# Where the first gate piece of a unit stands among the score products of a fused attention and feed-forward kernel

## The chip, the cores and the metric

The kernel runs on one core of a Trainium2 chip. The metric is the device time of one execution in microseconds (us); lower is better. Before the change the median of three executions is 332.06 us (331.29 to 332.46). The profiled execution took 331.38 us, and its trace spans 329.6 us from the first to the last instruction.

The engines are named as in the profile: PE is TensorE's matmuls, PEld its weight loads, ACT is ScalarE, DVE VectorE, POOL GpSimd, SP the engine that issues most transfers. L347 is line 347 of the kernel.

## The reference

An attention whose tokens attend only to tokens of the same cluster (the cluster of a token is the nearest of 16 centroids), followed by a SwiGLU feed-forward block on the normalised result. Four batches, 8 heads, 768 tokens, head size 64; model width 512, inner width 1536.

```python
q_assign = argmax(einsum('bhsd,hcd->bhsc', q_n, c_n), axis=-1)      # q_n, k_n, c_n: normalised rows
k_assign = argmax(einsum('bhsd,hcd->bhsc', k_n, c_n), axis=-1)
mask = q_assign[:, :, :, None] == k_assign[:, :, None, :]
scores = where(mask, scale * (q @ k.T), -1e9)
attn = softmax(scores)
x = (attn @ v)                       # reshaped to 3072 tokens x 512

xn = x / sqrt(mean(x * x) + 1e-6) * rms_g
g = xn @ w_gate
out = (g * sigmoid(g) * (xn @ w_val)) @ w_out
```

## The kernel before

The work is cut into 8 units, numbered 0 to 7: unit `u` is half of the query tokens (384) of one batch, for all 8 heads. A head of a unit has three *gaps*; in each, one pair of score matmuls is issued and its exponential taken. The one-hot cluster of a token is appended to its query and key (80 rows instead of 64), so that the mask comes out of the score product itself.

```python
def scores(u, h, i):
    ...
    ps = ps_s.tile([P, 2, 512], F32, tag="s", name="s")          # ps_s has 2 buffers in PSUM
    for j in range(n):                                            # n = 2: the pair
        nc.tensor.matmul(ps[:, j, :w], lhsT=cols(kext...), rhs=cols(qext...), start=True, stop=True)   # L347
    nc.scalar.activation(pT[u, h][:, n * i:n * i + n, :w], of, ACT.Exp, bias=off, ...)                # L351
```

`pv(u, h)` multiplies the exponentials of a finished head with the values (18 matmuls with 65 columns, L365), and after every second head normalises the result into `x` on VectorE (L370, L372). It runs one head late, after the second score pair of the next head. At a seam between units it is therefore the last head of unit `u - 1` that is multiplied after the second pair of unit `u`.

While the last head of a unit runs, ScalarE also squares the finished columns of `x` for the mean square, one of three pieces in each gap (`squares`, L392).

The feed-forward block of an earlier unit is cut into pieces. A gate or a value piece is four matmuls of 384 columns, into one of three PSUM buffers:

```python
def gv(u, f, val):
    ...
    full = ps_g.tile([P, UQ], F32, tag="gen", name="val" if val else "gate")    # ps_g has 3 buffers in PSUM
    for c in range(CC):
        nc.tensor.matmul(ps, lhsT=w[:, c, f * P:(f + 1) * P], rhs=xnT[u][:, c, :n], ...)               # L443
    if not val:
        th = gate.tile([P, UQ], F32, tag="th", name="th")[:, :n]
        nc.scalar.activation(th, ps, ACT.Tanh, scale=0.5)                                             # L451
        nc.vector.scalar_tensor_tensor(th, th, 1.0, ps, op0=ALU.add, op1=ALU.mult)                    # L452
    else:
        nc.vector.scalar_tensor_tensor(gvT[u][:, f, :n], gates[u], 0.5, ps, ...)                      # L456
```

(The last unit's gate and value products take another form; it is cut here.) The output product of a finished unit is cut into pieces in the same way (`out_mm`, L468), and the cluster products of the next group of heads too (L253).

`attention` writes the program of a unit: in each of its 24 gaps a score pair, in some a `pv`, and then pieces from the list `fill`, each with an estimated cost, so that they are spread evenly over the gaps:

```python
def attention(heads, fill, skip=0, hooks={}):
    gaps = [(u, h, i) for u, h in heads for i in range(UNITS[u][2])]
    total, done, n = sum(c for c, _ in fill), 0.0, 0
    for at, (u, h, i) in enumerate(gaps):
        scores(u, h, i)
        if i == (0 if (u, h) == (1, 0) else 1):
            for p in due:
                pv(*p)
            due[:] = [(u, h)]
        if h == H - 1:
            squares(u, i, False)
        ...
        while n < len(fill) and at >= skip and done <= total * (at + 1 - skip) / (len(gaps) - skip):
            done += fill[n][0]
            fill[n][1]()
            n += 1
```

From unit 2 on, `fill` begins with the last 8 gate and value pieces of unit `u - 2`; after them come the normalising of unit `u - 1`, the output pieces of unit `u - 2`, work for the next group of heads, and the first 16 gate and value pieces of unit `u - 1`. Units 2 to 5 skip the first gap, units 6 and 7 don't:

```python
    fill = ffn_work(u - 2)[CUT:] + [(0.0, lambda u=u: rms(u - 1))]                # CUT = 16 of 24
    rows, clusters = group(g)                                                     # g = u + 2
    ...
    attention([(u, h) for h in range(H)], fill, 1 if g < NG else 0)               # NG = 8
```

PE, ACT and DVE each take their instructions in the order in which the program issues them. The one-hot rows of a later group of heads are brought to their places in `kext` and `qext` by transfers that POOL issues (L296), behind a chain on DVE (cluster products transposed, the largest found, compared, transposed back).

Of the kernel before, what the change touches and what calls it, by code (L numbers as in the profile page):

```python
# [22 lines left out]
def kernel(  # L23
# [13 lines left out]
    B, H, S, D = q.shape  # L37
# [8 lines left out]
    NG = B * H // HG  # L46
# [158 lines left out]
    def load_o(c):  # L205
        nc.gpsimd.dma_start(out=wo[:, c:c + 4], in_=moe_w_out[c * P:(c + 4) * P].rearrange("(c p) f -> p c f", p=P))
# [130 lines left out]
    def scores(u, h, i):  # L337
        b, col, nt = UNITS[u]
        g, hh, w = b * 2 + h // HG, h % HG, nt * P
        if i == 0:  # L340
            pT[u, h] = ptp.tile([P, ST, UQ], BF16, tag="pT", name="pT")
        n = ST // nt
        ps = ps_s.tile([P, 2, 512], F32, tag="s", name="s")
        flat = ps.rearrange("p a b -> p (a b)")
        for j in range(n):
            kc = n * i + j
            nc.tensor.matmul(ps[:, j, :w] if nt == HT else flat[:, j * w:(j + 1) * w],  # L347
                             lhsT=cols(kext[g % 4][:KR, hh], g, kc // HT, kc % HT * P, (kc % HT + 1) * P),
                             rhs=cols(qext[g % 4][:KR, hh], g, col // HT, 0, w), start=True, stop=True)
        of = ps[:, :, :w] if nt == HT else flat[:, :n * w].rearrange("p (c w) -> p c w", w=w)  # L350
        nc.scalar.activation(pT[u, h][:, n * i:n * i + n, :w], of, ACT.Exp, bias=off, scale=scale if g >= BG else scale * ZS)  # L351
# [3 lines left out]
    def pv(u, h):  # L355
        b, _, nt = UNITS[u]
        g, hh = b * 2 + h // HG, h % HG
        if h == 0:
            xs[u] = xp.tile([P, HT, DM], F32, tag="x", name="x", bufs=2)
        if h % 2 == 0:  # L360
            accs[u] = ps_a.tile([P, 2, HT, D + 1], F32, tag="acc", name="acc")
        acc = accs[u]
        for t in range(nt):
            for kc in range(ST):
                nc.tensor.matmul(acc[:, h % 2, t], lhsT=pT[u, h][:, kc, t * P:(t + 1) * P],  # L365
                                 rhs=vbf[g % 4][:, hh, kc % HT * 2 + kc // HT], start=kc == 0, stop=kc == ST - 1)
        if h % 2:
            inv = small.tile([P, 2, HT], F32, tag="inv", name="inv")
            invs[u] = inv
            nc.vector.reciprocal(inv[:, :, :nt], acc[:, :, :nt, D])  # L370
            dst = xs[u][:, :nt, (h - 1) * D:(h + 1) * D].rearrange("p t (h d) -> p h t d", d=D)
            nc.vector.tensor_tensor(dst, acc[:, :, :nt, :D],  # L372
                                    inv[:, :, :nt].unsqueeze(3).broadcast_to([P, 2, nt, D]), op=ALU.mult)
# [8 lines left out]
    def squares(u, t, last):  # L382
        if (t, last) == (0, False):
            sq[u] = small.tile([P, 2, HT], F32, tag="ss", name="ss")
            xn[u] = xp.tile([P, CC, HT, P], BF16, tag="xn", name="xn")
        c = slice(CC - 1, CC) if last else slice(0, CC - 1)
        x, junk = by_chunk(xs[u][:, t])[:, c], xn[u][:, c, t]
        to = sq[u][:, int(last), t:t + 1]
        if u == 0:
            nc.vector.scalar_tensor_tensor(junk, x, 1.0 / DM, x, op0=ALU.mult, op1=ALU.mult, accum_out=to)  # L390
        else:
            nc.scalar.activation(junk, x, ACT.Square, scale=DM ** -0.5, accum_out=to)  # L392
# [95 lines left out]
    def group_work(g):  # L488

        t, c = [], []  # L490
        for h in range(HG):
            n = g * HG + h
            w = 0.0 if g >= BG else 0.3
            t += [(w, lambda h=h: trans(g, h, 0)), (w, lambda h=h: trans(g, h, 1))]

            def others(n=n):
                vcast(n)
                if n + NQ not in LATE:
                    load_qk(n + NQ)
                load_v(n + AV)  # L500

            def both(h=h, f=others):
                cast(nc.gpsimd, g, h, 0)
                f()
                cast(nc.gpsimd if g >= BG else nc.vector, g, h, 1, (0,))
            if g == 2:
                c.append((0.0, others))
            else:
                c += [(0.0, both), (0.0, lambda h=h: cast(nc.gpsimd if g >= BG else nc.vector, g, h, 1, (1,)))]
        a = []  # L510
        for m in range(2):
            a += [(0.0 if i else 0.7, f) for i, f in enumerate(cluster_steps(g, m))]
            if g == 3:
                a.append((0.0, lambda m=m: place(nc.gpsimd, g, m)))
            elif g == 2:
                a.append((0.0, (lambda: (place(nc.gpsimd, g, 1), place(nc.gpsimd, g, 0, (1,)))) if m else
                          (lambda: place(nc.gpsimd, g, 0, (0,)))))
        if g > 3:
            a[:1] = [(1.4, lambda f=(a[0][1], a.pop(4)[1]): [x() for x in f])]
            a.append((0.0, lambda: [place(nc.gpsimd, g, m) for m in range(2)]))  # L520
        return t, c, a

    def weave(t, c):

        return [x for pair in zip(t, c) for x in pair] + c[len(t):]
# [8 lines left out]
    def spread(a, b):  # L534

        if not a:
            return list(b)
        w, n = [], 0
        for i, x in enumerate(a):
            w.append(x)  # L540
            while n < len(b) * (i + 1) // len(a):
                w.append(b[n])
                n += 1
        return w

    def ffn_work(u):
        n = UNITS[u][2] / HT
        return [(0.64 * n, lambda f=f, val=val: gv(u, f, val)) for f in range(FC) for val in (False, True)]

    def out_work(u):  # L550
        return [(0.86, lambda t=t, p=p: out_mm(u, t, p)) for t in range(UNITS[u][2]) for p in range(3)]
# [103 lines left out]

    due = []

    def attention(heads, fill, skip=0, hooks={}):
        gaps = [(u, h, i) for u, h in heads for i in range(UNITS[u][2])]
        total, done, n = sum(c for c, _ in fill), 0.0, 0  # L660
        for at, (u, h, i) in enumerate(gaps):
# [6 lines that stand above are left out]
                squares(u, i, False)  # L668
            if (u, h, i) in hooks:
                hooks[u, h, i]()  # L670
            while n < len(fill) and at >= skip and done <= total * (at + 1 - skip) / (len(gaps) - skip):
                done += fill[n][0]
                fill[n][1]()
                n += 1
        for _, f in fill[n:]:
            f()

    attention([(0, h) for h in range(H)], [], hooks={(0, *divmod(i, HT)): f for i in range(H * HT) for f in [first.get(i, more)] if f})
    for u in range(1, NU):
        ffn, o, g = ffn_work(u - 1), out_work(u - 2) if u > 1 else [], u + 2  # L680
        if u == 1:
            t, c, a = group_work(2)
            t3, c3, a3 = group_work(3)
            n = LEAD - 4
            o3 = [(0.0, lambda i=i: load_o(i)) for i in range(0, FC, 4)]
            prep = c + a + spread(weave(t3[n:], c3), o3) + a3[:5]
            idle = const.tile([P, 1], BF16)

            def norm():
                rms(0)  # L690
                nc.gpsimd.tensor_copy(idle, xn[0][:, CC - 1, HT - 1, P - 1:])
                for h in range(HG):
                    casts(pool_, H + h, K0, Q0, K1, Q1)

            hooks = {(1, 0, 0): late[6], (1, 0, 1): lambda: (late[7](), norm())}
            hooks.update({(1, *divmod(2 + i, HT)): t3[i][1] for i in range(n)})
            hooks[1, *divmod(LEAD - 1, HT)] = lambda: xtrans_all(0)
            fill = spread(ffn[:CUT], prep)
            attention([(1, h) for h in range(H)], fill, LEAD, hooks)
        else:  # L700
            fill = ffn_work(u - 2)[CUT:] + [(0.0, lambda u=u: rms(u - 1))]
            rows, clusters = group(g)
            fill += [(0.0, lambda n=n: load_qk(n)) for n in LATE if n // HG == u + 3]
            if u == 2:
                fill += spread(o[:3], [(0.0, f) for _, f in a3[5:]])
                o = o[3:]
            fill += spread(o, rows) + spread(ffn[:CUT], clusters)
            attention([(u, h) for h in range(H)], fill, 1 if g < NG else 0)
    rest = ffn_work(NU - 2)[CUT:]
    rest[0][1]()  # L710
    pv(NU - 1, H - 1)
# [38 lines left out]
```

The softmax here doesn't subtract the row's maximum and nothing guards it: scores larger than these inputs give would overflow.

## Time and profile before

| | before |
|---|---|
| median of 3 executions | 332.06 us |
| span of the trace | 329.6 us |
| PE busy | 320.9 us (97%) |
| ACT busy | 247.8 us (75%) |
| DVE busy | 223.7 us (68%) |
| POOL busy | 136.3 us (41%) |
| DMA, mean over the span | 104 GB/s |
| matmuls | 2877 |

A busy time is the sum of the intervals in which an engine has an instruction recorded. A group line of the page names the line, the engine, the operation, what it writes and reads, and how many there are; behind the bar stand the busy time, the mean duration of one in ns, and the idle time of the engine just before these instructions with what ended it. A line of a timeline gives the start and the length in us, then the engine, the line, the operation and how many in a row were merged; in brackets stands the idle time before it and what ended it.

The chain of waits that ended last lies on PE for 77% of the span, on DVE for 10% and on ACT for 6%.

### The profile page before, as it was taken

How to read it: one execution, taken by the hardware profiler on the slowest of the kernel's cores; microseconds unless marked ns; L12 is line 12 of the kernel's file. 1: busy time of each engine (PE TensorE's matmuls, PEld its weight loads, DVE VectorE, ACT ScalarE, POOL GpSimd, SP SyncE). 2: the span in 40 equal slices, each digit the busy share in tenths (PEclk: the TensorE clock that was granted, in tenths of full speed). 3: DMA queues.
4: the chain of work that ended last, by engine and by line, in shares of the span. 5: the costliest groups of instructions: out<-in, count | busy, mean ns of one | idle time of the engine just before them, and what ended most of it. 6: DMA issues, size and time to landing. Idle time of an engine off the chain costs nothing.

```text
span 329.6 us, 7822 instructions
## 1 busy us (share of the span) xinstructions
PE 320.9 (97%) x2877; PEld 192.8 (58%) x2877; DVE 223.7 (68%) x508; ACT 247.8 (75%) x429; POOL 136.3 (41%) x273
## 2 busy tenths in 40 slices
PE   8999899999999999999999999999999999999995
PEld 4647557564466655665566555665566656655653
DVE  6999976968777685877678694976265635684430
ACT  5899979986679867897778876797779868853331
POOL 6999499950977156440926247350000000000000
PEclk9999999999999999999999999999999999999999
DMA  7999995894546344561546640000600040002002
GB/s 266 367 263 241 255 201 108 129 198 112 89 92 142 104 69 74 118 150 52 97 74 131 161 111 34 6 21 1 146 2 0 2 111 34 2 1 95 2 1 97
DMA packets 82919, 34.25 MB, mean 104 GB/s; under 512 B 64064, under 2 KB 79808, under 8 KB 82880
## 3 DMA queue, kind: packets, MB, share of 16 engines
q1 hardware_dynamic: 73712, 27.44, 34.4%
q0 software_dynamic: 8880, 5.91, 10.9%
q8 instruction: 23, 0.38, 0.5%
q10 hardware_dynamic: 288, 0.39, 0.4%
q14 instruction: 16, 0.13, 0.1%
HBM read 28.61 MB, written 6.29 MB: 106 GB/s over the span
## 4 chain that ended last, share of the span: by engine, by line
PE 77%; DVE 10%; ACT 6%; SPq 3%; issue 2%; DMA 1%; POOL 0%; DVEq 0%; ACTq 0%; POOLq 0%
PE o L468 18%; PE gate L443 15%; PE val L443 15%; PE s L347 15%; PE acc L365 8%; ACT pT L351 3%; SPq L95 3%; PE sc L253 2%; DMA qk<-in_k_dram 1%; ACT xn L392 1%; ACT th L451 1%; DVE kext L331 1%; DVE qext L331 1%; PE warm L131 1%; DVE pads L326 1%
## 5 line engine op out<-in xcount | busy, mean ns | idle before, releaser
L351 ACT ACTIVATE pT<-s,off 128x768 bf16<-128x768 f32 x192 | 171.0, 905 | 32.2 <-PE s L347 31.6
L347 PE MATMUL s<-qext,kext 80*128 80x384 bf16 x384 | 94.8, 328 | 2.7 <-ACT pT L351 1.9
L443 PE MATMUL gate<-xnT,wg 128*128 128x384 bf16 x384 | 78.3, 326 | 0.1
L443 PE MATMUL val<-xnT,wv 128*128 128x384 bf16 x384 | 78.1, 326 | 0.0
L452 DVE SCALAR_TENSOR_TENSOR th<-th,gate 128x384 f32<-128x384 f32 x84 | 46.2, 550 | 36.6 <-ACT th L451 36.1
L468 PE MATMUL o<-wo,gvT 128*128 128x512 bf16 x276 | 68.1, 379 | 0.0
L347 PEld LDWEIGHTS <-kext 80*128 80x128 bf16 x384 | 36.3, 98 | 37.0 <-issue 9.1
L456 DVE SCALAR_TENSOR_TENSOR gvT<-th,val 128x384 bf16<-128x384 f32 x84 | 46.5, 553 | 10.2 <-PE val L443 3.1
L451 ACT ACTIVATE th<-gate 128x384 f32<-128x384 f32 x84 | 41.2, 490 | 15.1 <-PE gate L443 14.3
L443 PEld LDWEIGHTS <-wg 128*128 128x128 bf16 x384 | 36.0, 97 | 23.0 <-issue 0.8
L365 PEld LDWEIGHTS <-pT 128*128 128x128 bf16 x1152 | 43.4, 97 | 10.0 <-DVE x L372 1.1
L443 PEld LDWEIGHTS <-wv 128*128 128x128 bf16 x384 | 36.0, 97 | 22.4
L239 POOL CAST qext<-qkT 64x384 bf16<-64x384 f32 x64 | 35.5, 561 | 32.7 <-DVE inv L370 20.4
L365 PE MATMUL acc<-vbf,pT 128*128 128x65 bf16 x1152 | 45.7, 193 | 0.6 <-ACT pT L351 0.2
L468 PEld LDWEIGHTS <-gvT 128*128 128x128 bf16 x276 | 25.8, 97 | 26.0 <-issue 0.6
L296 POOL DMA_DIRECT2D qext<-oh x48 | 23.1, 491 | 27.0 <-DVE oh L285 22.5
L239 POOL CAST kext<-qkT 64x384 bf16<-64x384 f32 x54 | 29.4, 545 | 4.0 <-DVE qkT L224 2.2
L296 POOL DMA_DIRECT2D kext<-oh x48 | 23.0, 488 | 14.7 <-DVE oh L285 14.6
L471 ACT COPY o_sb<-o 128x512 f32<-128x512 f32 x23 | 13.5, 586 | 15.8 <-PE o L468 15.8
L370 DVE RECIPROCAL inv<-acc 128x6 f32<-128x6 f32 x32 | 6.0, 189 | 22.6 <-PE acc L365 22.0
L372 DVE TENSOR_TENSOR x<-acc,inv 128x384 f32<-128x384 f32 x32 | 17.8, 557 | 1.1
L242 POOL CAST vbf<-vs 128x384 bf16<-128x384 f32 x32 | 16.6, 527 | 1.6
(83 smaller groups left out, 235.4 us busy)
## 6 DMA issues: line engine op xcount, KB each, us to landing
vs<-in_v_dram SPq DMA_DIRECT2D x32, 192.0 KB, 4.2
out_dram<-o_sb SPq DMA_DIRECT2D x23, 256.0 KB, 2.5
qk<-in_q_dram SPq DMA_DIRECT2D x16, 192.0 KB, 4.2
qk<-in_q_dram SPq DMA_DIRECT2D x64, 48.0 KB, 2.7
qk<-in_k_dram SPq DMA_DIRECT2D x64, 48.0 KB, 2.6
qk<-in_k_dram SPq DMA_DIRECT2D x14, 192.0 KB, 4.4
wg<-in_moe_w_gate_dram POOLq DMA_DIRECT2D x4, 384.0 KB, 8.8
wv<-in_moe_w_val_dram POOLq DMA_DIRECT2D x4, 384.0 KB, 11.4
```

The source lines that it names most:

```text
L239: on.tensor_copy(to, of)
L242: nc.gpsimd.tensor_copy(vbf[n // HG % 4][:, n % HG, :, :D], stagedv[n])
L296: on.dma_start(out=ext[D:D + NC, h, e * UQ:(e + 1) * UQ], in_=put[g, m][32 * h + e * NC:32 * h + (e + 1) * NC])
L347: nc.tensor.matmul(ps[:, j, :w] if nt == HT else flat[:, j * w:(j + 1) * w], lhsT=cols(kext[g % 4][:KR, hh], g, kc // HT, kc % HT * P, (kc ...
L351: nc.scalar.activation(pT[u, h][:, n * i:n * i + n, :w], of, ACT.Exp, bias=off, scale=scale if g >= BG else scale * ZS)
L365: nc.tensor.matmul(acc[:, h % 2, t], lhsT=pT[u, h][:, kc, t * P:(t + 1) * P], rhs=vbf[g % 4][:, hh, kc % HT * 2 + kc // HT], start=kc == 0 ...
L372: nc.vector.tensor_tensor(dst, acc[:, :, :nt, :D], inv[:, :, :nt].unsqueeze(3).broadcast_to([P, 2, nt, D]), op=ALU.mult)
L443: nc.tensor.matmul(ps, lhsT=w[:, c, f * P:(f + 1) * P], rhs=xnT[u][:, c, :n], start=c == 0, stop=c == CC - 1)
L451: nc.scalar.activation(th, ps, ACT.Tanh, scale=0.5)
L452: nc.vector.scalar_tensor_tensor(th, th, 1.0, ps, op0=ALU.add, op1=ALU.mult)
L456: nc.vector.scalar_tensor_tensor(gvT[u][:, f, :n], gates[u], 0.5, ps, op0=ALU.mult, op1=ALU.mult)
L468: nc.tensor.matmul(outs[u], lhsT=gvT[u][:, f, t * P:(t + 1) * P], rhs=wo[:, f], start=f == 0, stop=f == FC - 1)
```

## The change

The change gives `attention` a new argument, `ahead`: that many pieces of `fill` may be issued before the skipped gaps are over. With `ahead=1`, the first piece of units 2 to 5 (a gate piece of unit `u - 2`) is issued in the first gap, between the first two score pairs of the unit, where before nothing stood between them. It is there to give PE work while the second pair waits for its buffer.

```diff
-    def attention(heads, fill, skip=0, hooks={}):
+    def attention(heads, fill, skip=0, hooks={}, ahead=0):
...
-            while n < len(fill) and at >= skip and done <= total * (at + 1 - skip) / (len(gaps) - skip):
+            while n < len(fill) and (n < ahead or at >= skip) and done <= total * (at + 1 - skip) / (len(gaps) - skip):
...
-            attention([(u, h) for h in range(H)], fill, 1 if g < NG else 0)
+            attention([(u, h) for h in range(H)], fill, 1 if g < NG else 0, ahead=1)
```

On PE the four gate matmuls of each of the four units move ahead of the second score pair and the `pv` behind it. On ACT the tanh of that gate comes between the first two exponentials of the unit, where it came behind the second. On DVE its product comes ahead of the reciprocal and the normalising of `x` instead of behind them. The programs of POOL and SP are the same.

## The prediction

> **What bounds the kernel now.** I read the page first for the engines' shares, then a table of stages, then the timelines of TensorE (PE) and ScalarE (ACT) at the seams between two units. The page:
>
> ```profile
> PE 320.9 (97%) x2877; PEld 192.8 (58%) x2877; DVE 223.7 (68%) x508; ACT 247.8 (75%) x429; POOL 136.3 (41%) x273
> L351 ACT ACTIVATE pT<-s,off 128x768 bf16<-128x768 f32 x192 | 171.0, 905 | 32.2 <-PE s L347 31.6
> L347 PE MATMUL s<-qext,kext 80*128 80x384 bf16 x384 | 94.8, 328 | 2.7 <-ACT pT L351 1.9
> ```
>
> TensorE is the busy engine, and the exponentials of ScalarE wait for it (31.6 us in all) far more than it waits for them (1.9 us). That 1.9 us is the change's target. A matmul's recorded end is modelled, so its busy share flatters it; I therefore go by starts. Four 384-column matmuls of a gate or value piece start 0.65 us before the next group (gate at 105.40, val at 106.05 below), though each is recorded as 326 ns: the pace is 0.163 us per matmul. A pair of score matmuls takes 0.33 us, a `pv` of 18 matmuls 0.55 us.
>
> The table of stages, cut where the first score pair of each of the units 2 to 7 starts (columns: length, then busy time and instructions of PE, PEld, DVE, ACT, POOL, then clock, DMA share, GB/s):
>
> ```profile
> 65.10:103.77 38.67, 38.38 (x350) 22.23 (x348) 29.93 (x67) 29.51 (x52) 23.79 (x48) 1.00 0.71 132
> 103.77:141.36 37.59, 37.32 (x343) 22.24 (x340) 27.45 (x62) 29.51 (x52) 17.48 (x36) 1.00 0.47 93
> ...
> 216.54:252.18 35.64, 35.64 (x326) 21.89 (x325) 19.61 (x46) 29.19 (x52) 3.82 (x8) 1.00 0.16 38
> ```
>
> Units 3, 4 and 5 take 37.59 us each, units 6 and 7 take 35.64. PE has 0.27 us of idle time in each of the former and none in the latter. The timeline of PE from unit 2 into unit 3 (columns: start, length, operation, number in the run, idle time before it) shows where:
>
> ```profile
> 103.29 0.65 PE L443 MATMUL val<-xnT,wv 128*128 128x384 bf16 x3
> 103.77 0.49 PE L347 MATMUL s<-qext,kext 80*128 80x384 bf16 x2
> 104.53 0.48 PE L347 MATMUL s<-qext,kext 80*128 80x384 bf16 x2 [0.27 <-ACT pT L351]
> 104.85 0.71 PE L365 MATMUL acc<-vbf,pT 128*128 128x65 bf16 x18
> 105.40 0.81 PE L443 MATMUL gate<-xnT,wg 128*128 128x384 bf16 x4
> 106.05 0.81 PE L443 MATMUL val<-xnT,wv 128*128 128x384 bf16 x4
> ```
>
> The second score pair starts 0.76 us after the first, where 0.33 would do. So 0.43 us are lost, more than the printed 0.27, as the modelled tail of the first pair hides the rest. ScalarE at that time:
>
> ```profile
> 103.56 0.91 ACT L351 ACTIVATE pT<-s,off 128x768 bf16<-128x768 f32 x1
> 104.35 0.54 ACT L392 ACTIVATE xn<-x 128x384 bf16<-128x384 f32 x1
> 104.76 0.22 ACT L392 ACTIVATION_READ_ACCUMULATOR xn<-x 128x1 f32 x1
> 104.85 1.71 ACT L351 ACTIVATE pT<-s,off 128x768 bf16<-128x768 f32 x2
> ```
>
> The exponential that ends at 104.47 is that of the last score pair of the unit before; it frees the score buffer (there are two), and 0.06 us later the stalled pair starts. ScalarE is late because the three squarings of the seam (0.54 us and a read-out each) stand between the exponentials of the last head. The same seam into unit 6, where a gate and a value piece already stand between the two pairs, has no gap:
>
> ```profile
> 216.54 0.49 PE L347 MATMUL s<-qext,kext 80*128 80x384 bf16 x2
> 216.86 0.81 PE L443 MATMUL gate<-xnT,wg 128*128 128x384 bf16 x4
> 217.51 0.81 PE L443 MATMUL val<-xnT,wv 128*128 128x384 bf16 x4
> 218.16 0.49 PE L347 MATMUL s<-qext,kext 80*128 80x384 bf16 x2
> 218.49 0.71 PE L365 MATMUL acc<-vbf,pT 128*128 128x65 bf16 x18
> ```
>
> **What the Trainium skill says.** "Perfetto Trace Analysis", Tensor Engine Instruction: the end time of a matmul is estimated, the start is when it begins to read; this agrees with 0.33 us recorded at a 0.163 us pace, and is why I measure gaps from start to start. The same page, Optimization Strategy: look for the gaps on the contended engine and for what blocks there; here that is one release, four times. "TensorE: Matmul & The Clock Gate", Architectural detail (the array is 16× 32×32): matmuls keep program order and only weight loads are pulled ahead, while ScalarE and VectorE are strict queues. The trace agrees for PE: the seam's third weight load is done by 104.03, 0.50 us before the matmul that uses it. So PE cannot pass the blocked pair by itself: the order in the program must do it.
>
> **The change part by part.** It removes and adds no instruction. In each of units 2, 3, 4 and 5 one gate piece (4 matmuls, 0.65 us) moves from behind the `pv` to between the first two score pairs. Its tanh on ScalarE moves from behind the second exponential of the unit to ahead of it, and its product on VectorE from behind the normalising of `x` to ahead of it. Units 6 and 7 already start without the skip, so the new argument does nothing there; the later pieces keep their places, as the running total of costs is unchanged.
>
> The seam into unit 3, worked anew: first pair at 103.77, gate at 104.10, second pair at 104.75. Its release comes at 104.53, so it no longer waits, with 0.22 us to spare. `pv` at 105.07, val at 105.62 instead of 106.05. Gain: 0.43 us. The other seams have the same gaps: pairs at 65.10 and 65.86, at 141.36 and 142.12, at 178.95 and 179.70. Sum: 0.43 + 0.43 + 0.43 + 0.42 = 1.71 us, about 1.7.
>
> A second way to it gives the same: unit 3 is 37.59 - 35.64 = 1.95 us longer than unit 6. Its 16 cluster matmuls take the PE from 126.13 (behind a pair at 125.80) to 127.65, 1.52 us. What is left is 0.43 us.
>
> All of it lies on the path that sets the end: outside that gap the PE timeline of unit 3 is closed, start to start, and units 6, 7 and the tail follow in PE's order. I expect the span to go from 329.60 to about 327.9.
>
> **Rivals.**
> 1. The moved piece makes a new wait by ScalarE's order. At the seam into unit 6 the tanh starts 1.86 us after the first pair, the second exponential 2.23 us after. For unit 3 that is tanh at 105.63, exponential from 106.00 to 106.94. The pair that needs the buffer of this exponential is the fourth, now at 108.33 - 0.43 = 107.90: 0.9 us to spare. The third needs the first exponential's (over at about 105.7) and starts at 106.27. Against this rival, then; were it true, up to the whole 1.7 us would go.
> 2. A wait for one of the three PSUM buffers of gates and values. The moved gate takes the buffer whose value at this seam was read long before. The tightest is the second gate behind it: it needs the buffer of the moved gate's value, read on VectorE behind product, reciprocal and normalising, by my count from 107.34 to 107.89 (the steps of these on VectorE being 0.47, 0.22 and 0.48 us from start to start), against a start at 108.66 - 0.43 = 108.23. Some 0.3 us to spare; a loss of 0.1 to 0.2 us a seam is possible.
> 3. A transfer that doesn't move with PE. In unit 2 the first scores of the second head group wait for the one-hot rows:
>
> ```profile
> 84.83 0.11 PEld L347 LDWEIGHTS <-kext 80*128 80x128 bf16 x2 [0.51 <-DMA kext<-oh]
> ```
>
> Start to start, PE loses 0.18 us there (four `o` matmuls take 0.87 us, 82.59 to 83.46 on the timeline; 83.79 + 0.87 = 84.66, the pair starts at 84.84). If that landing stays where it is, unit 2's 0.43 us is given back there and 1.3 us remain, 330.8. But its chain starts on VectorE with a step that itself waited 0.45 us for ScalarE, which follows PE; I expect it to move along for the most part.
> 4. Nothing measurable: the three times before lie 331.29 to 332.46, 1.2 us apart. The gain is only a little more than this.
>
> **Range and chances.** 332.06 - 1.7 = 330.36; I allow 0.1 for rivals 2 and 3 and call it 330.4. The spread of single times makes 0.5 us either way for a median likely, and rival 3 pulls upward: 329.5 to 331.4. Two per cent is 6.6 us, four times the idle time addressed, so faster by over 2% cannot come from this mechanism. Slower by over 2% would need 1.7 us more in every one of the four units, and nothing in the margins above is near it.
>
> **What would show each step right or wrong.** Right: at the four seams the order pair, gate, pair, `pv` with starts 0.33, 0.65 and 0.33 us apart and no wait on ScalarE's `pT`; PE's waits for `pT` down from 1.9 us to about 0.8 (four of 0.27 gone); units 3, 4 and 5 at 37.16 us, units 6 and 7 still 35.64. Wrong: a gap before the second gate behind the moved one (rival 2), before the third or fourth pair (rival 1), or a wait on the rows in unit 2 that has grown from 0.18 to about 0.6 us (rival 3). What would make the number wrong with the mechanism right is a shift of whole executions of some 0.3%, which no step of this sum covers.

## The result and the profile after

| | before | after |
|---|---|---|
| median, first measurement (4 executions each) | 331.98 us | 330.04 us |
| median, measured again (22 and 12 executions) | 332.00 us | 330.45 us |
| span of the trace | 329.6 us | 328.0 us |

The ratio of the times is 0.9942 (95% interval 0.9914 to 0.9969) in the first measurement and 0.9949 (0.9931 to 0.9968) in the second. The medians differ by 1.9 and by 1.6 us, and the second ratio, the one with more executions behind it, stands for 1.7 us. Both intervals stay below 1: a gain of half a per cent, far inside two per cent.

The page of the changed kernel, engines and the same two group lines:

```profile
PE 319.8 (98%) x2863; PEld 193.0 (59%) x2877; DVE 222.8 (68%) x508; ACT 247.5 (75%) x429; POOL 136.2 (42%) x273
L351 ACT ACTIVATE pT<-s,off 128x768 bf16<-128x768 f32 x192 | 171.1, 906 | 30.9 <-PE s L347 30.3
L347 PE MATMUL s<-qext,kext 80*128 80x384 bf16 x384 | 94.8, 328 | 1.6 <-ACT pT L351 0.8
```

The waits of the score pairs for the exponential fell from 1.9 to 0.8 us: those at the four seams are gone, three in units 0 and 1 are left. (PE shows 2863 matmuls instead of 2877 because 14 records of output matmuls are missing from this trace; their weight loads, 2877, are all there. So PE's busy time is about 0.1 us too low in each of the units 2 to 6 and 0.2 us in the last, and nothing can be read from that.)

The timeline of PE at the seam from unit 2 into unit 3:

```profile
102.92 0.81 PE L443 MATMUL val<-xnT,wv 128*128 128x384 bf16 x4
103.57 0.49 PE L347 MATMUL s<-qext,kext 80*128 80x384 bf16 x2
103.90 0.81 PE L443 MATMUL gate<-xnT,wg 128*128 128x384 bf16 x4
104.55 0.49 PE L347 MATMUL s<-qext,kext 80*128 80x384 bf16 x2
104.88 0.71 PE L365 MATMUL acc<-vbf,pT 128*128 128x65 bf16 x18
105.42 0.81 PE L443 MATMUL val<-xnT,wv 128*128 128x384 bf16 x4
106.07 0.49 PE L347 MATMUL s<-qext,kext 80*128 80x384 bf16 x2
```

The starts lie 0.33, 0.65 and 0.33 us apart, the pace of the matmuls themselves, and no bracket follows. Before, the `val` piece started 2.28 us behind the first pair (103.77 to 106.05), now 1.85 us: 0.43 us less for the same 26 matmuls. The table of stages, from first pair to first pair of units 2 to 7:

```profile
65.38:103.57 38.19, 38.08 (x347) 22.23 (x348) 29.79 (x67) 29.39 (x52) 23.74 (x48) 1.00 0.72 133
103.57:140.74 37.17, 37.06 (x341) 22.23 (x341) 27.29 (x62) 29.41 (x52) 17.46 (x36) 1.00 0.49 96
...
215.07:250.71 35.64, 35.53 (x324) 21.89 (x325) 19.62 (x46) 29.20 (x52) 3.82 (x8) 1.00 0.16 38
```

Unit 3 takes 37.17 us instead of 37.59, units 4 and 5 the same, unit 6 still 35.64. The account of the whole span: the first pair of unit 2 came 0.28 us later in this execution, units 2 to 5 took 149.69 us instead of 151.44 (1.75 less), and the rest 112.96 instead of 113.06: 0.28 - 1.75 - 0.10 = -1.57 us, the difference of the spans (328.03 and 329.60).

### The profile page after: what moved, and what is told of

Its sections match the earlier page's. It is cut to its first block, busy times and chain, and to the rows that moved or that the text cites. A ratio compares the mean times of both kernels' runs of the same rounds, so it can differ in the third digit from the quotient of the medians.

```text
span 328.0 us, 7804 instructions
## 1 busy us (share of the span) xinstructions
PE 319.8 (98%) x2863; PEld 193.0 (59%) x2877; DVE 222.8 (68%) x508; ACT 247.5 (75%) x429; POOL 136.2 (42%) x273
## 4 chain that ended last, share of the span: by engine, by line
PE 87%; DVE 9%; ACT 2%; issue 1%; POOL 0%; DVEq 0%; ACTq 0%; POOLq 0%
PE gate L443 18%; PE val L443 18%; PE o L468 18%; PE s L347 17%; PE acc L365 9%; PE sc L253 3%; DVE kext L331 1%; DVE qext L331 1%; PE warm L131 1%; DVE pads L326 1%; DVE qkT L224 1%; PE tq L220 1%; PE o L479 1%; ACT pT L351 1%; DVE xn L390 1%
## 5 line engine op out<-in xcount | busy, mean ns | idle before, releaser
L468 PE MATMUL o<-wo,gvT 128*128 128x512 bf16 x262 | 66.5, 378 | 0.8
L392 ACT ACTIVATE xn<-x 128x384 bf16<-128x384 f32 (+1 forms) x42 | 17.3, 415 | 0.0
```

Source lines behind the costliest of these rows:

```text
L468: nc.tensor.matmul(outs[u], lhsT=gvT[u][:, f, t * P:(t + 1) * P], rhs=wo[:, f], start=f == 0, stop=f == FC - 1)
```

## The experiments

In all of them I read the length of the units, from first pair to first pair, which repeats to 0.01 us between executions of different kernels (unit 6 took 35.63 or 35.64 us in every one). Unit 2 is the exception: it holds a wait for the transferred one-hot rows, which differs from execution to execution (rival 3 below). The span doesn't repeat so well either: it begins with transfers, so that the first score pair of the program comes at 10.2 to 11.2 us, and it ends with one.

**Half of the change.** The early piece in units 3 and 5 only.

```diff
-            attention([...], fill, 1 if g < NG else 0, ahead=1)
+            attention([...], fill, 1 if g < NG else 0, ahead=1 if u in (3, 5) else 0)
```

> The changed kernel, with the early gate piece in units 3 and 5 only; units 2 and 4 keep their old order. Theory (each seam is a hole of 0.43 us that the piece fills, and the holes add up): units 3 and 5 37.17 us from first pair to first pair as in the changed kernel, unit 4 37.59 and unit 2 about 38.6 as before; a span of about 328.8, half of the gain. Rival (the gain is one shift that the whole program settles into, wherever it starts): units 2 and 4 change too, or the gain is all or nothing.

The table of stages, units 3, 4, 5:

```profile
104.85:142.01 37.16, 37.16 (x341) 22.23 (x340) 27.26 (x62) 29.37 (x52) 17.46 (x36) 1.00 0.46 93
142.01:179.59 37.58, 37.32 (x342) 22.22 (x340) 27.44 (x62) 29.48 (x52) 17.46 (x36) 1.00 0.49 101
179.59:216.76 37.17, 37.17 (x343) 22.23 (x341) 27.26 (x62) 29.37 (x52) 17.47 (x36) 1.00 0.28 75
```

The units with the piece are the short ones, and nothing spreads from one to the next. Unit 2 took 38.75. Yet the span was 330.3 us, above that of the kernel before, where 328.8 was expected: the first pair of unit 2 came at 66.10 instead of 65.10, and the last stretch was half a microsecond longer. The single execution took 332.11 us beside 331.74 for the kernel before. Read by its time alone, half of the gain would have looked like a loss.

**How large is the hole?** The kernel before, with matmuls on constants put between the first two pairs of units 2 to 5, two (0.43 us) and then four (0.87 us). Their results are not used (they go into one of the three PSUM buffers of gates and values); the gate piece stays in its old place.

```diff
             if (u, h, i) in hooks:
                 hooks[u, h, i]()
+            if at < skip == 1:
+                busy(2, False)          # and busy(4, False)
             while n < len(fill) and at >= skip and ...
```

> The kernel before, with two matmuls of 512 columns on constants (0.43 us of TensorE, results not used) between the first two score pairs of units 2 to 5; the gate piece stays where it was. Theory (TensorE stands idle there for 0.43 us): they are free, units 3 to 5 stay at 37.59 us within 0.03, the span at 329.6. Rival (the first pair's tail or the weight load holds the second pair, so that the hole cannot be used): each of the three units gets up to 0.43 us longer, about 38.0.

> The kernel before, with four such matmuls (0.87 us) at the same four places. Theory (the hole is 0.43 us and no more): half of them is free and half is paid, units 3 to 5 at 38.02 us, the span about 331.3. Rival of a larger hole (another 0.2 to 0.4 us hidden behind the pv or a later wait): under 37.8 us.

The seam into unit 4 in the timelines of PE, with two matmuls and then with four:

```profile
141.63 0.49 PE L347 MATMUL s<-qext,kext 80*128 80x384 bf16 x2
141.96 0.59 PE L131 MATMUL warm<-warm 128*128 128x512 bf16 x2
142.40 0.49 PE L347 MATMUL s<-qext,kext 80*128 80x384 bf16 x2
```

```profile
142.66 0.49 PE L347 MATMUL s<-qext,kext 80*128 80x384 bf16 x2
142.98 1.03 PE L131 MATMUL warm<-warm 128*128 128x512 bf16 x4
143.85 0.49 PE L347 MATMUL s<-qext,kext 80*128 80x384 bf16 x2
```

Two fit exactly: the pairs stand 0.77 us apart, as they did with nothing between them (0.76 us), and units 3 to 5 took 37.59, 37.60 and 37.60 us. With four, units 3 to 5 took 38.03 us each, 0.44 more than before. So the hole is 0.43 us of TensorE that matmuls other than the gate piece fill just as well, and no more of it is hidden further on.

**Is the order on TensorE enough?** The changed order of the matmuls, but the tanh and the product of the moved gate left behind the second exponential and the normalising of `x`.

```diff
+            if at == 0 and first:
+                first()                 # units 2 to 5: the gate's four matmuls alone
             while n < len(fill) and at >= skip and ...
                 fill[n][1]()            # its tanh and product, in the first piece's old place
```

> The changed kernel's order on TensorE (the four gate matmuls between the first two pairs of units 2 to 5), but the tanh of this gate and its product stay behind the second exponential and the normalising of x, as in the kernel before. Theory with the count of PSUM buffers: the exponential then starts at about 105.43 on the clock of the changed kernel, the tanh at 106.2, the product ends at 107.3, and the second value piece, which takes the same PSUM buffer and is due at 107.05, waits about 0.3 us: units 3 to 5 at about 37.45 us, and of the 0.43 us of each seam some 0.13 remain; the wait shows ahead of the second value piece. Rival (only the order on TensorE matters, the buffers have room): 37.17 us as in the changed kernel.

The timeline of PE at the seam into unit 4:

```profile
142.83 0.71 PE L365 MATMUL acc<-vbf,pT 128*128 128x65 bf16 x18
143.38 0.81 PE L453 MATMUL val<-xnT,wv 128*128 128x384 bf16 x4
144.03 0.49 PE L347 MATMUL s<-qext,kext 80*128 80x384 bf16 x2
144.35 0.81 PE L453 MATMUL gate<-xnT,wg 128*128 128x384 bf16 x4
145.33 0.81 PE L453 MATMUL val<-xnT,wv 128*128 128x384 bf16 x4 [0.16 <-DVE th L444]
```

and of DVE (L444 is the moved gate's product in this kernel):

```profile
143.81 0.56 DVE L372 TENSOR_TENSOR x<-acc,inv 128x384 f32<-128x384 f32 x1
144.72 0.55 DVE L444 SCALAR_TENSOR_TENSOR th<-th,gate 128x384 f32<-128x384 f32 x1 [0.35 <-ACT th L443]
```

The seam itself is closed, but two pieces later TensorE waits: the second value piece starts at 145.33 instead of 145.00, when the product that frees its PSUM buffer is over at 145.27. Units 3 to 5 took 37.49, 37.48 and 37.49 us. Of the 0.43 us, 0.32 were given back. Filling TensorE's hole is thus not enough: with the tanh in its old place three quarters of the gain go. It is the tanh that is late here, not the order on VectorE, since the product waits 0.35 us for it with nothing else to do.

**Why is there a hole?** The kernel before, with the three squarings at the end of units 1 to 4 on VectorE.

```diff
     def squares(u, t, last):
         ...
-        if u == 0:
+        if u == 0 or u < 5 and not last:
             nc.vector.scalar_tensor_tensor(junk, x, 1.0 / DM, x, ..., accum_out=to)
```

> The kernel before, with the three squarings at the end of units 1 to 4 on VectorE instead of ScalarE. The prediction said that these squarings make ScalarE late at the seam. By the count of the trace they can only be part of it: without them the last exponential of the unit before could start when its score pair is done (about 103.33 on the clock of the kernel before) and end at 104.24, and the second pair, due at 104.10, would start at 104.30 instead of 104.53. So units 3 to 5 at about 37.36 us: 0.23 of the 0.43 us are the squarings, 0.20 are the exponential itself. Rival (the squarings are the whole cause): 37.16 us. Rival (VectorE, in order, gets late and holds PSUM buffers): 37.6 us or more.

The seam into unit 4 in the timelines of PE and ACT, then unit 2 on PE:

```profile
142.58 1.04 PE L347 MATMUL s<-qext,kext 80*128 80x384 bf16 x4
143.46 0.71 PE L365 MATMUL acc<-vbf,pT 128*128 128x65 bf16 x18
142.19 2.67 ACT L351 ACTIVATE pT<-s,off 128x768 bf16<-128x768 f32 x3
...
70.32 0.81 PE L443 MATMUL val<-xnT,wv 128*128 128x384 bf16 x4 [0.92 <-DVE th L452]
```

The two pairs are merged into one line of four matmuls; the `pv` starts 0.88 us behind the first of them, where 0.65 would do, so 0.23 us of the hole are left (1.08 to 0.88 us: 0.20 gone). Units 3 to 5 took 37.38 us, against 37.36 expected. So the squarings are half of the cause; the other half is that an exponential of 0.9 us cannot end in the time in which TensorE has only one value piece and one pair to do. The last one of unit 3 starts at 142.19, 0.59 us behind the start of its own pair (141.60), and is over at about 143.09; the second pair starts at 143.13. A tanh still stands ahead of that exponential, but it can hold it by 0.06 us at most: with ScalarE idle before it, an exponential started 0.53 us behind its pair (106.70 and 107.23 in the kernel before). And in unit 2 the other rival came true as well: VectorE, with more to do, freed a PSUM buffer too late, by 0.92 us in the bracket and 1.08 us from start to start, so that unit 2 took 39.61 us. The span of 330.4 us, 0.8 above the kernel before, is only in part that: the first pair of unit 2 came half a microsecond later.

**Do the two remedies add?** The changed kernel with the squarings on VectorE too (the same edit).

> The changed kernel with the squarings of the seams on VectorE as well. Theory (both remove the same wait, so they do not add): units 3 to 5 at 37.17 us. If they added, 36.94 us.

Units 3 to 5 took 37.16, 37.17 and 37.17 us. They remove the same wait and don't add. In unit 2 the squarings on VectorE cost something here too: it took 38.64 us, and TensorE waits 0.31 and 0.18 us, from start to start, ahead of a value and a gate piece where the changed kernel has no wait.

**More than one early piece.** First `ahead=2`, then, as that turned out to be the changed kernel again, an edit that lets two pieces through.

> The changed kernel with two early pieces, a gate and a value piece, in units 2 to 5. Theory (the hole of 0.43 us is filled by the first piece of 0.65 us): nothing more to gain, units 3 to 5 at 37.17 us within 0.03. Rival (room left at the seam): shorter units. Rival (the value piece delays the pv and the last normalising): longer ones.

With one cost of 0.64 on the running total, the condition on that total is false in the skipped gap, so `ahead=2` issues one piece as well; the program was the same. As a repetition it gave 37.16, 37.17 and 37.16 us for units 3 to 5, and 328.5 us of span.

```diff
-            while n < len(fill) and (n < ahead or at >= skip) and done <= total * (...) / (...):
+            while n < len(fill) and (n < ahead or at >= skip and done <= total * (...) / (...)):
...
-            attention([...], fill, 1 if g < NG else 0, ahead=1)
+            attention([...], fill, 1 if g < NG else 0, ahead=2)
```

> The changed kernel with a gate and its value piece between the first two pairs of units 2 to 5 (the run before this one with the same aim left the limit of the running total in force, which let only one piece through, so it was the changed kernel again). Theory (one piece of 0.65 us more than fills the hole of 0.43): the second pair starts 1.63 us after the first instead of 0.98, and units 3 to 5 stay at 37.17 us within 0.03. Rival (a value piece ahead of the pv makes ScalarE or VectorE late, or meets a full PSUM buffer): longer units. Rival (room left at the seam): shorter ones.

The second pair started 1.63 us behind the first, and units 3 to 5 took 37.17, 37.17 and 37.16 us: no gain, and no cost.

**The same kind of wait elsewhere.** In the changed kernel's last stretch a gate piece starts 0.24 us late:

```profile
288.84 0.81 PE L443 MATMUL val<-xnT,wv 128*128 128x384 bf16 x4
289.73 0.81 PE L443 MATMUL gate<-xnT,wg 128*128 128x384 bf16 x4
```

The start to start of 0.89 us against 0.65 is the only sign; the modelled tail of the value piece leaves no bracket. The edit gives the last three gates the score buffers, free by then:

```diff
+        if u == NU - 2 and f >= CUT // 2 + 1 and not val:
+            full = ps_s.tile([P, UQ], F32, tag="s", name="gate")
+        else:
             full = ps_g.tile([P, UQ], F32, tag="gen", name="val" if val else "gate")
```

> The changed kernel, with the last three gate pieces of unit 6, which run after the last score pair, in the two score buffers that are free by then, instead of the three buffers for gates and values. In the changed kernel the gate piece at 289.73 starts 0.24 us behind the end of the value piece before it, with its first weights loaded, and two later ones some 0.03 us. Theory (these are waits for a PSUM buffer): the gaps go, from the first output piece on the program stands 0.3 us earlier against the last seam, a span of about 327.7 at the same start; in the timed rounds about 0.3 us below the changed kernel, within their scatter. Rival (VectorE's order sets this stretch): no change.

The same two pieces in that kernel's timeline:

```profile
289.16 0.81 PE L446 MATMUL val<-xnT,wv 128*128 128x384 bf16 x4
289.81 0.81 PE L446 MATMUL gate<-xnT,wg 128*128 128x384 bf16 x4
```

From the first pair of unit 7 to the first matmul of the last output product, PE took 70.61 us instead of 70.88 (70.60 and 70.88 in the executions below). The gap was a PSUM buffer. The first times, 330.35 us in four executions (ratio to before 0.9957, 0.9940 to 0.9974), don't show it. So both kernels ran again, one after the other on one chip:

> The changed kernel once more, on the same chip as the next run and in five rounds. Theory (four holes of 0.43 us, 1.7 us in all; the rest of the 1.9 us first measured is scatter of the start and of the last transfer): 1.7 us below the kernel before, a ratio of 0.995. Units 3 to 5 at 37.17 us again, whatever the start of unit 0 is. If more than the holes is gained, the ratio stays at 0.994 and some stretch outside the seams is shorter.

> The changed kernel with the last three gate pieces of unit 6 in the score buffers, beside the changed kernel itself. By the traces it should be 0.27 us faster from the first pair of unit 7 to the last output product; the scatter of single executions is about three times that, so a difference of medians between -0.6 and +0.3 us would fit.

The changed kernel: 330.45 us, the ratio given at the start. With the tail edit: 330.01 us, 0.9932 (0.9913 to 0.9952). The intervals of the two overlap widely. That the tail edit gains 0.27 us is seen in the traces; that it gains time beyond the scatter is not.

## Why the prediction was right, point by point

- **The wait at the seam, 0.43 us, four times.** Right in place and in size. The two matmuls on constants fitted exactly, the four cost the difference.
- **A start-to-start reading instead of the printed idle time.** Right: the bracket says 0.27 us, the units became 0.42 us shorter. The brackets alone would have given 1.1 us instead of 1.7.
- **All of it lies on the path.** Right: 1.75 us in units 2 to 5 and nothing given back behind them. Unit 2 gained 0.48 us in this pair of traces; 0.05 us of that is chance, as its wait for the one-hot rows happened to be shorter too.
- **Rival 1, ScalarE's order.** It did not come: no bracket behind the seam, and the exponential ran from 105.80 on a clock that is 0.2 us ahead, as worked out.
- **Rival 2, PSUM buffers.** It did not come in the changed kernel: the buffer counted as the tightest was free at 107.69, and the piece that needs it started at 108.03, 0.34 us later, about the 0.3 worked out. The run with the late tanh shows that the danger was real: on the buffer of the moved gate itself, that order costs 0.32 us of 0.43. The line of VectorE that frees the buffer in the changed kernel:

```profile
107.15 0.54 DVE L456 SCALAR_TENSOR_TENSOR gvT<-th,val 128x384 bf16<-128x384 f32 x1
```

- **Rival 3, the transfer in unit 2.** It did not come. In the trace of the changed kernel the pair starts 0.13 us late (84.64 against 83.64 + 0.87 = 84.51) instead of 0.18, but one pair of traces cannot show this, as the wait differs by itself: 0.18, 0.26 and 0.32 us in three traces with nothing put between the first two pairs of unit 2 or with two matmuls that fit, and 0.13 to 0.35 us in six with early pieces. With this wait taken off, unit 2 lasts 38.48 to 38.50 us in those three and 38.06 or 38.07 us in those six. So its seam, too, gave 0.43 us, and the wait of about 0.6 us that would have swallowed them was in none.
- **"ScalarE is late because the three squarings stand between the exponentials."** Only half right, the one step that a run corrected. Without the squarings 0.20 of the 0.43 us went, and 0.23 stayed, as the last exponential simply has too little matmul work beside it. The sum did not depend on this step, since the filler closes the hole whatever made it.
- **The time.** 330.4 was said; 330.04 and 330.45 were measured. That they lie so close is in part luck, as single executions of one kernel lie 1.2 us apart.

## What to carry to other kernels

On an engine that works through its program in order, look for a repeated start-to-start gap and put work there that depends on nothing near; anything that fits is free up to the size of the gap, and beyond it is paid in full. Follow the moved piece to the end: what frees its buffer must move with it, or the wait comes back two pieces later. And judge a change of a few tenths of a microsecond by the length of a stretch that repeats, not by the time of the whole program.

## What was not expected of the hardware

Stretches in the middle of this program repeat to 0.01 us between kernels (unit 6: 35.63 or 35.64 us every time), while the wait for the rows in unit 2 (0.09 to 0.35 us), the start and the end scatter: the first score pair came between 10.16 and 11.23 us, and the stretch behind the first pair of unit 7 took 77.33 and 77.52 us in two executions of the same kernel. The end scatters only behind the last matmul. From the first pair of unit 7 to the start of the last matmul TensorE took 73.46 to 73.48 us in all traces but the two of the tail edit (73.20); from there to the end of the span it was 3.3 to 4.5 us, of which the last copies out of PSUM take 0.5. What is left are the last transfers of the output and the end of the program. Most of the 1.2 us between the slowest and the fastest time of one kernel can come from the start and from there; which transfer is the cause was not followed up.
